# Weights of two modes in one load, and Q, K and V loaded in runs of 36 tokens

## The chip, the cores and the metric

The kernel runs on one core of a Trainium2 chip. The metric is the device time of one execution in microseconds (us); the kernel before has a median of 426.58 us over 9 runs (426.47 to 427.04). PE is TensorE (matmuls, and transposes made as matmuls), DVE is VectorE, ACT is ScalarE, POOL is GpSimd and SP is SyncE. In this kernel POOL issues all loads and SP most of the stores; the transfers themselves run on 16 DMA engines.

## The reference, cut to what matters

Inputs are q, k and v (8 batches, 8 heads, 576 tokens, 64 channels, fp32), the weights w_r and w_i (64 modes of 512x512, fp32) and w_ch (512x512). The first half is causal attention with a window of 64 tokens:

```python
scores = scale * np.matmul(q, k.transpose(0, 1, 3, 2))
mask = (rel >= 0) & (rel < window)          # rel: query position less key position, window 64
attn = softmax(where(mask, scores, -1e9))
x = np.matmul(attn, v)                       # then (batch, token, head*64 + channel)
```

The second half mixes the 64 lowest frequencies along the tokens with a complex weight for each, and then the channels:

```python
X = np.fft.rfft(x, axis=1)
Yr = einsum('bmd,mde->bme', Xr, w_r) - einsum('bmd,mde->bme', Xi, w_i)
Yi = einsum('bmd,mde->bme', Xr, w_i) + einsum('bmd,mde->bme', Xi, w_r)
y = np.fft.irfft(Y, n=S, axis=1)             # Y is zero from mode 64 on
u = x + y
return u + np.maximum(u @ w_ch, 0.0)
```

The weights are 127 matrices of 1 MiB in fp32 (mode 0 needs no imaginary one); they are cast to bf16 by the load, so that one takes 512 KB of SBUF, 4 KB in each partition.

## The kernel before, in words

**Attention** goes batch by batch. `load` (L95) brings K, Q or V of one batch into a raw tile with one DMA; a partition holds two runs of `RUN` = 18 tokens, one of a head in the first half of the heads and one of a head in the second. `transpose_units` (L205) makes twelve units of each batch: nine parts (three each for K, V and Q), in which PE transposes a third of the run's tokens into a PSUM tile `pst` and ACT or DVE copies it out (L218, L221), and three `vback` units that turn V back. PE's and POOL's orders are written out by hand here: for every window `w` come the scores (L291), the weighing of the window before (L316), the masks (L272) and in between the units that are due, three to a window, and the Fourier transforms of finished batches (`dft`, `dft_turn`).

**Loads during attention.** After a part has freed a raw tile, `refill` (L375) issues the raw load of two batches later, and with it one weight (`early`, L354). The first 5 weights (`LW`) go to the pool `wlate`, 13 more (`EW`) to `wearly`, and at the end 15 to tiles of attention that have come free (`spare`, L362). So 33 weights, those of modes 0 to 16, are issued before the modes begin.

**The modes.** `mode(m)` (L566) multiplies the transformed activations XQ of mode m with its real and then its imaginary weights, four matmuls of 512 columns each (L575), and after each half calls `refill_w` (L518), which takes places that have come free and issues the next weights into them with `load_w` (L110). Places are the five tiles of `wlate`, eight of `wmid` (`mids`, L494) that lie where attention's tiles lay and close again from mode 48 on, when their memory is wanted for the spectra `Y` (`batch_tile`, L705), one `wx` from mode 48 on, and three parts of `wy` from mode 54 on. A list `opens` says from which mode a place may be used, and its last field up to which. All loads stand in one queue behind POOL; a load waits there for the place that it fills, and for the landing of the load eight before it, whose semaphore it uses again.

From mode 17 to 47 PE has other work between the modes, the channel products `Z` (L597, L609). For modes 0 to 47 the order on PE is found by the planner of the framework; from mode 48 on it is by hand again, with the inverse transforms of the spectra (L724, L726) and the last four modes in another form (`last_mode`, L775). After the last weight, `YT2` is filled, turned, and the output rows are summed, rectified and stored (L885, L890, L908).

The softmax here doesn't subtract the row's maximum and nothing guards it: scores larger than these inputs give would overflow.

## Time and profile before

| What | Value |
|---|---|
| median of 9 runs | 426.58 us |
| the profiled execution's own time | 426.47 us |
| its span, first to last instruction | 424.7 us |
| mean granted clock of TensorE | 0.939 |
| PE busy | 360.1 us (85%) |
| DVE, ACT, POOL busy | 184.7, 171.5, 89.5 us |
| DMA packets | 28646, 91.98 MB |
| raw loads | 24 of 576 KB |
| weight loads | 127 of 512 KB |

The profile is of one execution, on one core. Its page lists busy times by engine, the span in 40 slices of 10.6 us each (GB/s is what the DMA engines wrote), the DMA queues, the chain of work that ended last, and the costliest groups of instructions. Further answers of the trace give who waited for whom (us in total, times, longest), the chain in order of time (start, length, what) and the timeline of an engine. [...] Landing records say when a load had arrived. The loads of all weights are issued at L115, and those of Q, K and V at L97.

### The profile page before, as it was taken

How to read it: one execution, taken by the hardware profiler on the slowest of the kernel's cores; microseconds unless marked ns; L12 is line 12 of the kernel's file. 1: busy time of each engine (PE TensorE's matmuls, PEld its weight loads, DVE VectorE, ACT ScalarE, POOL GpSimd, SP SyncE). 2: the span in 40 equal slices, each digit the busy share in tenths (PEclk: the TensorE clock that was granted, in tenths of full speed). 3: DMA queues.
4: the chain of work that ended last, by engine and by line, in shares of the span. 5: the costliest groups of instructions: out<-in, count | busy, mean ns of one | idle time of the engine just before them, and what ended most of it. 6: DMA issues, size and time to landing. Idle time of an engine off the chain costs nothing.

```text
span 424.7 us, 8859 instructions
## 1 busy us (share of the span) xinstructions
PE 360.1 (85%) x3762; PEld 219.6 (52%) x3772; DVE 184.7 (44%) x397; ACT 171.5 (40%) x314; POOL 89.5 (21%) x171
## 2 busy tenths in 40 slices
PE   6989998998998899467698979999858986589993
PEld 5655765665665465212265646555334443256682
DVE  5566756766764201404542422333113432140994
ACT  4585865866863311201132313122113332130993
POOL 7231231331122142222222222221222132200000
PEclk9999999999996699966799998999999999959998
DMA  8999999999999999999999999999999999994598
GB/s 144 212 213 212 214 212 214 213 213 213 214 214 213 214 213 262 212 213 214 212 215 213 215 212 214 213 213 214 212 215 213 214 213 214 214 212 100 189 387 333
DMA packets 28646, 91.98 MB, mean 217 GB/s; under 512 B 2832, under 2 KB 3088, under 8 KB 28608
## 3 DMA queue, kind: packets, MB, share of 16 engines
q0 software_dynamic: 25344, 81.80, 96.6%
q1 hardware_dynamic: 3120, 9.50, 5.8%
q8 instruction: 29, 0.48, 0.4%
q10 hardware_dynamic: 144, 0.13, 0.1%
q14 instruction: 9, 0.07, 0.0%
HBM read 162.53 MB, written 9.44 MB: 405 GB/s over the span
## 4 chain that ended last, share of the span: by engine, by line
DMA 48%; PE 37%; DVE 8%; issue 2%; ACT 2%; POOL 1%; DVEq 0%; POOLq 0%
DMA wt<-in_moe_w_r_dram 36%; DMA wt<-in_moe_w_i_dram 7%; PE pso L316 7%; PE pst L218 6%; DMA wch<-in_moe_w_ch_dram 4%; PE pso L885 4%; PE psv L235 3%; DVE x_sb L324 3%; PE psx L338 3%; PE pss L371 2%; PE pss L272 2%; PE psy L575 2%; PE pss L291 2%; DVE vT L59 2%; PE pso L769 1%
## 5 line engine op out<-in xcount | busy, mean ns | idle before, releaser
L575 PE MATMUL psy<-wt,XQ 128*32 128x512 bf16 (+1 forms) x404 | 96.1, 407 | 31.9 <-DMA wt<-in_moe_w_i_dram 17.1
L575 PEld LDWEIGHTS <-XQ 128*32 128x32 bf16 x476 | 48.5, 131 | 77.1 <-issue 57.1
L604 DVE CAST xT<-pxt 128x256 fp32r<-128x256 bf16 (+1 forms) x68 | 26.3, 434 | 53.6 <-PE pxt L597 33.8
L115 POOL DMA_DIRECT2D wt<-in_moe_w_r_dram x54 | 29.0, 538 | 93.2 <-DMA wt<-in_moe_w_r_dram 44.3
L611 ACT CAST Z<-psz 128x512 fp32r<-128x512 f32 x36 | 21.1, 587 | 66.4 <-PE psz L609 66.3
L115 POOL DMA_DIRECT2D wt<-in_moe_w_i_dram x52 | 27.9, 537 | 81.1 <-DMA wt<-in_moe_w_i_dram 43.6
L297 ACT ACTIVATE et<-pss 128x512 bf16<-128x512 f32 x72 | 39.2, 599 | 13.2 <-PE pss L291 13.2
L609 PE MATMUL psz<-wch,xT 128*128 128x512 f32 x144 | 42.2, 429 | 0.9 <-DVE xT L604 0.9
L316 PE MATMUL pso<-vt,et 128*64 128x65 bf16 (+1 forms) x576 | 34.0, 209 | 5.2 <-DVE x_sb L324 5.1
L609 PEld LDWEIGHTS psz<-wch,xT 128*128 128x128 f32 x144 | 27.1, 200 | 15.1 <-issue 8.8
L316 PEld LDWEIGHTS <-et 128*64 128x64 bf16 (+1 forms) x576 | 23.7, 113 | 17.2 <-issue 9.8
L59 DVE COPY x_sb<-psy 128x256 f32<-128x256 f32 x15 | 6.4, 424 | 57.0 <-PE psy L575 57.0
L324 DVE TENSOR_TENSOR x_sb<-pso,rcp 128x640 bf16<-128x640 f32 x32 | 26.3, 822 | 0.9
L58 ACT COPY x_sb<-psy 128x256 f32<-128x256 f32 x15 | 5.6, 374 | 50.5 <-DVE x_sb L59 50.5
L885 PE MATMUL pso<-Y,trigI 128*128 128x512 f32 x80 | 23.1, 403 | 0.1
L908 DVE TENSOR_TENSOR ot<-pso,x_sb 128x512 f32<-128x512 f32 x35 | 22.2, 685 | 1.5 <-PE pso L885 1.1
L272 PE MATMUL pss<-band,ident_bf 64*64 64x512 bf16 x136 | 20.2, 407 | 1.5 <-ACT et L297 1.5
L59 DVE CAST x_sb<-psj 128x512 bf16<-128x512 f32 x18 | 12.2, 688 | 21.2 <-PE psj L786 18.3
L59 DVE COPY vT<-pst 128x768 bf16<-128x768 bf16 x16 | 15.3, 958 | 13.0 <-PE pst L218 13.0
L890 ACT ACTIVATE pso<-pso 128x512 f32<-128x512 f32 x36 | 19.1, 596 | 0.0
L58 ACT CAST x_sb<-psj 128x512 bf16<-128x512 f32 x18 | 10.6, 586 | 19.6 <-PE psj L786 19.6
L885 PEld LDWEIGHTS pso<-Y,trigI 128*128 128x128 f32 x80 | 14.5, 188 | 5.5 <-ACT pso L890 1.7
(157 smaller groups left out, 506.4 us busy)
## 6 DMA issues: line engine op xcount, KB each, us to landing
wt<-in_moe_w_r_dram POOLq DMA_DIRECT2D x54, 512.0 KB, 19.1
wt<-in_moe_w_i_dram POOLq DMA_DIRECT2D x52, 512.0 KB, 19.1
out_dram<-ot SPq DMA_DIRECT2D x15, 512.0 KB, 4.1
rk<-in_k_dram POOLq DMA_DIRECT2D x8, 576.0 KB, 9.6
rq<-in_q_dram POOLq DMA_DIRECT2D x8, 576.0 KB, 13.6
rv<-in_v_dram POOLq DMA_DIRECT2D x8, 576.0 KB, 12.2
wy<-in_moe_w_r_dram POOLq DMA_DIRECT2D x3, 512.0 KB, 17.7
wy<-in_moe_w_i_dram POOLq DMA_DIRECT2D x3, 512.0 KB, 19.1
```

What stands on the lines that cost most here:

```text
L59: return nc.vector.tensor_copy(out=o, in_=i)
L115: nc.gpsimd.dma_start(out=wt, in_=src[m].rearrange("(p c) e -> p c e", c=NC))
L218: nc.tensor.transpose(out=ps[64 * hh:64 * hh + 64, c, :], in_=src[:, hh, (c0 + c) * D:(c0 + c + 1) * D], identity=ident_bf)
L272: nc.tensor.matmul(out=pss[(2 * w + hh) % 3][64 * half:64 * half + 64, :], lhsT=ident_bf[pp, pp], rhs=view(band[pp], 128 * half, [[0, WIN ...
L297: nc.scalar.activation(out=et[:, hh, :], in_=pss[(2 * w + hh) % 3], func=ACT_F.Exp, scale=EX_SCALE)
L316: nc.tensor.matmul(out=pso[po, hh, (i // 2) * VW:(i // 2) * VW + D + 1], lhsT=et[pk, hh, col:col + 64], rhs=vt[pk, 1 - f % 2, 2 * hh + g / ...
L324: nc.vector.tensor_tensor(out=view(x_sb, b * NT * DM + g * D, [[4 * D, 2], [DM, NT], [1, D]]), in0=view(pso, 0, [[512, 2], [VW, NT], [1, D]]),
L575: nc.tensor.matmul(out=psy[r0:r0 + k, :], lhsT=xq(c, m, im, [[NM, k]]), rhs=w[:, c, :], start=(im + c == 0), stop=(im == (m > 0) and c == ...
L604: nc.vector.tensor_copy(out=xT[:, :, w * k:w * k + w], in_=view(psts[k], j, [[128, NC], [n, w]] if n > 1 else [[128, NC], [1, 64], [64, 2]]))
L609: nc.tensor.matmul(out=psz, lhsT=xT[:, c, :], rhs=wch[:, c, :], start=(c == 0), stop=(c == NC - 1))
L885: nc.tensor.matmul(out=tps[n], lhsT=trigI[:, tr:tr + 128], rhs=pair_tile(what, bb), start=False, stop=stop and r0 + k == 128, skip_group_c ...
L908: nc.vector.tensor_tensor(out=ot[:, j], in0=ps, in1=x_sb[:, b, t, :], op=ALU.add)
```

## The change

`RUN` becomes 36 tokens, so that a partition holds one run of one head, 64 partitions the first four heads and 64 the others; a batch of K is one block of memory read from end to end. A part still covers a third of the run, now `CP` = 12 tokens, with a transpose of 64 partitions by 64 channels for each token and half of the heads, 24 in place of 12.

The pool `wlate` is cut into two double places `WP` and a single one `W1`, and `wmid` into four double ones. `load_two` brings the weights of modes m and m+1 (both real, or both imaginary) in one DMA into a double place. The list `items` holds 30 such pairs for modes 17 to 46 and 34 single loads for modes 47 to 63. `refill_w` gives the next item the first free place that fits; a double place is split into two single ones when the next item is single. A pair's place comes free when the second of its modes is done. The tiles `Y` of the spectra are now shared by two batches.

```diff
-    RUN = S // 32
+    RUN = S // 16
+    CP = RUN // 3
...
+    WP = [wlate.tile([128, 2, NC, DM], BF16, name="wt", tag=f"wp{j}") for j in range(LW // 2)]
+    W1 = wlate.tile([128, NC, DM], BF16, name="wt", tag="w1")
...
-            out=r, in_=RAW[which][b].rearrange("(x g) (p c) d -> (g p) x (c d)", g=4, c=RUN))
+            out=r, in_=RAW[which][b].rearrange("h (p c) d -> (h p) (c d)", c=RUN))
...
+    def load_two(m, im, wt):
+        src = moe_w_i if im else moe_w_r
+        nc.gpsimd.dma_start(out=wt, in_=src[m:m + 2].rearrange("m (p c) e -> p m c e", c=NC))
+        for j in range(2):
+            wtiles[m + j, im] = wt[:, j]
...
-                ps = ps_misc.tile([128, 6, 128], BF16, name="pst", tag="misc")
-                for c in range(6):
+                ps = ps_misc.tile([128, CP, 64], BF16, name="pst", tag="misc")
+                for c in range(CP):
                     for hh in range(2):
-                        nc.tensor.transpose(out=ps[64 * hh:64 * hh + 64, c, :],
-                                            in_=src[:, hh, (c0 + c) * D:(c0 + c + 1) * D],
-                                            identity=ident_bf)
-                evac(view(dst, c0, [[S, 4], [RUN, 32], [1, 6]]),
-                     view(ps, 0, [[32, 4], [1, 32], [128, 6]]), on_act)
+                        pp = slice(64 * hh, 64 * hh + 64)
+                        nc.tensor.transpose(out=ps[pp, c, :], in_=src[pp, (c0 + c) * D:(c0 + c + 1) * D],
+                                            identity=ident_bf[pp, pp])
+                evac(view(dst, c0, [[S, 4], [RUN, 16], [1, CP]]),
+                     view(ps, 0, [[16, 4], [1, 16], [64, CP]]), on_act)
...
-    MW = 8
+    MW = 4
-    mids = {j: wmid.tile([128, NC, DM], BF16, name="wt", tag=f"wm{j}") for j in range(MW)}
+    mids = [wmid.tile([128, 2, NC, DM], BF16, name="wt", tag=f"wm{j}") for j in range(MW)]
...
+    M2, M1 = mode_of(nw), M0 - 1
+    items = [(m, im, True) for m in range(M2, M1, 2) for im in range(2)]
+    items += [(m, im, False) for m in range(M1, NM) for im in range(2)]
+    for j, wt in enumerate(WP):
+        opens.setdefault(mode_of(2 * j + 1), []).append((wt, True, NM))
+    opens.setdefault(mode_of(LW - 1), []).append((W1, False, ME - 3))
+    for j, wt in enumerate(mids):
+        at = mode_of(LW + EW + 1 - 2 * j) if j else vt_mode
+        opens.setdefault(at, []).append((wt, True, M0 + 2 * j))
...
+        while items:
+            m1, im1, two = items[0]
+            fit = [s for s in free if (s[1] or not two) and s[2] > m1 + two]
+            if not fit:
+                break
+            wt, pair, last = slot = fit[0]
+            at = free.index(slot)
+            free.pop(at)
+            items.pop(0)
+            if two:
+                load_two(m1, im1, wt)
+                slot_of[m1 + 1, im1] = slot
                 continue
+            if pair:
+                free.insert(at, (wt[:, 1], False, last))
+                slot = (wt[:, 0], False, last)
+            load_w(2 * m1 - 1 + im1, None, None, slot[0])
+            slot_of[m1, im1] = slot
...
-            Yp[b] = wmid.tile([128, 2, DM], FP32R, name=f"Y{b}", tag=f"wm{b}")
+            Yp[p] = wmid.tile([128, 2, 2, DM], FP32R, name=f"Y{p}", tag=f"wm{p}")
```

## The prediction

> **What bounds the kernel now.** I read the page's busy times, slices and queues first, then the waits, then the chain of work in order of time, then POOL's and PE's timelines.

> ```profile
> span 424.7 us, 8859 instructions
> GB/s 144 212 213 212 214 212 214 213 213 213 214 214 213 214 213 262 212 213 214 212 215 213 215 212 214 213 213 214 212 215 213 214 213 214 214 212 100 189 387 333
> q0 software_dynamic: 25344, 81.80, 96.6%
> q8 instruction: 29, 0.48, 0.4%
> HBM read 162.53 MB, written 9.44 MB: 405 GB/s over the span
> ```

> From slice 2 to slice 36 the loads write 212 to 215 GB/s without a break (the 262 is the one load that isn't cast). They read fp32 and write bf16, so that is some 427 GB/s read. By the landing records the first raw load lands at 6.76 us, the last weight at 389.94. No other engine is as full: PE is busy 85%.

> Next, the waits of POOL, which issues all the loads, and pieces of the chain (start, length, what):

> ```profile
> POOL wt L115 <- DMA wt<-in_moe_w_r_dram: 53.3, 26, 3.9
> POOL wt L115 <- DMA wt<-in_moe_w_i_dram: 50.8, 27, 3.8
> POOL wt L115 <- PE psy L575: 43.9, 18, 6.5
> ...
> 170.73 18.98 DMA wt<-in_moe_w_r_dram
> 314.08 19.14 DMA wt<-in_moe_w_r_dram
> 350.90 19.13 DMA wt<-in_moe_w_i_dram
> 370.08 1.88 PE psy L575 x4
> 390.21 0.49 PE psl L775 x16
> ```

> POOL mostly waits for the landing of the load eight issues back, not for a free place; about 19 us of transfers stand queued. The end is set so: the stream of loads to 389.9, then 34.8 us of work on PE, DVE and ACT after the last weight. A change counts if it alters the stream's rate, lets it run dry, or alters that tail.

> **Where it could run dry** is the handover from attention to modes:

> ```profile
> 141.48 0.54 POOL L115 DMA_DIRECT2D vt<-in_moe_w_i_dram  x1
> 148.51 0.53 POOL L115 DMA_DIRECT2D wt<-in_moe_w_r_dram  x1 [6.50 <-PE psy L575]
> ```

> The load of 141.48 lands at 155.26. A load's first byte needs about 2.7 us after issue (the first load: issued 1.25, landed 6.76, its transfer 2.78), so the one issued at 148.51 was ready by 151.2: 4.05 us of slack. In attention the raw loads wait on transposes, with slack of 3.4 us (issued 23.81, the one ahead landing at 29.91) and 3.6 us (39.53, 45.79) at the tightest.

> [...]from a 128x64 transpose to a 64x64 score 149 ns pass between starts, of which the 128 columns need 53, so some 95 ns a switch. [...]

> **The change part by part.**

> *Raw loads.* 24 loads go from 256 packets of 2304 B to 128 of 4608 B. Single packets took 192 ns (2304 B) and 324 ns (4096 B): the line through both has 22 ns fixed. But packets overlap: all together fill 410 us of an engine (96.6% of the span) in 386 us of stream. By landings a raw load alone takes 2.783 us for 576 KB, a weight load 2.458 us for 512 KB: only 0.65% more a byte. Removing that: 24 x 2.783 x 0.0065 = -0.43 us. Bounds: 0, and 192 x 22 ns = -4.3 us if each fixed part counted in full. I take -0.4.

> *First load.* POOL's first raw issue takes 0.83 us, a weight's 0.53; half the packets should start the stream about 0.2 us sooner (0 to -0.4).

> *Pairs.* Modes 17 to 46 have 60 loads; they become 30. Bytes and packets (two of 4096 B a partition) stay; 30 completions of 22 ns go: -0.66 in full, -0.15 if they overlap as data does; I take -0.3. Two packets a partition is the shape of the raw loads, which ran at full rate.

> *More PE instructions.* A part has 24 transposes instead of 12: 8 batches x 9 parts x 12 x 2 (weight load and matmul) = 1728 more. The 7534 PE records and q8's 0.48 MB give 64 B each, so 0.11 MB, 7 fetches of 16 KB more. One holds a DMA engine 0.61 us (16,384 B at 26.7 GB/s); their times repeat in a cycle of eight, so I take eight engines in turn: 7/8 x 0.61 = +0.5 us on the slowest (0 to +0.6).

> Stream: -0.4 - 0.2 - 0.3 + 0.5 = -0.4 us.

> *Transposes on PE.* The pace of matmuls with 64-column weights (start, length, engine, what):

> ```profile
> 46.76 0.41 PE L291 MATMUL pss<-qT,kT 64*64 64x128 bf16 x15
> 47.10 0.44 PE L316 MATMUL pso<-vt,et 128*64 128x65 bf16 x14
> 59.15 0.84 PE L218 MATMUL pst<-ident_bf,rq 128*64 128x128 bf16 x24
> ```

> The 24 transposes of the last line are two parts, 12 pairs whose halves run side by side; 0.62 us from first to last start is 56 ns a pair, set by 128 columns. After, two parts are 24 pairs of 64 columns. The weighing matmuls L316 (65 columns, two column halves) are nearest: the second pair comes 53 ns after the first[...], later pairs 29 to 36, mean 32. So 53 + 22 x 32 + 27 = 784 ns against 11 x 56 + 53 = 669: +115 ns, x 36 = +4.1 us over attention. Against it, 64x64 is the shape of scores (L291) and masks (L272). Taking PE's order of before and giving L218 the new shape, mode switches fall from 316 to 292: 24 x 95 ns = -2.3 us. Evacuations wait for the last matmul, whose modelled length falls from 219 to about 194 ns: 36 x 25 = -0.9. Net +0.9 us. Bounds: pairs at 28 ns (the scores' mean) give 36 x 27 ns - 3.2 = -2.2; at 53 ns always, 36 x 605 ns - 3.2 = +18.6.

> What hides +0.9 is the slack of 4.05 us. The change takes 1.0 of it, since the first refill opens after mode 1's imaginary half, not mode 0, and the quicker stream 0.6: 2.5 us are left. Beyond that each us is a us of the end. Evacuations keep 768 elements a partition (813 ns ACT, 958 DVE); I put them at nothing, between -0.1 and +0.1 us each, with the same cover.

> *Places.* Modes 17 to 46 have six double places, where before there were 13 single ones; W1 stands idle till mode 47. Every load now waits on a place, so the question is the queue's depth. PE's worst lag: weights of mode 32 (imaginary) landed at 236.4, were done at 246.5. With pairs the four next pair loads and one issued at 238.7 would be queued or landed, to 261: 14.5 us, less 2.7 of latency, is 11.8 us of slack. From mode 47 the counts are the old ones (4 + 1 + 1 + 3), where the tightest issue (337.36, the one ahead landing at 347.92) had 7.9 us. So nothing, covered by queue depth; each us beyond would cost a us.

> *Tail.* The shared Y tiles are written before either batch of a pair is read in it; its instructions stay. Nothing.

> Sum: 424.7 - 0.4 = 424.3; around the span lie 1.8 us (426.47 profiled); the median is 0.11 above: 426.2 us.

> **Rivals.** *Slower: transposes.* If two pairs' weight loads don't overlap ([...]the first pair of each L316 run speaks for it, later pairs against), attention ends 18.6 us later and the stream stands dry for 16: 442. At 40 ns a pair: +291 ns x 36 - 3.2 = 7.3, less 2.5: +4.8, 431. It decides from 35.5 ns a pair: net +3.8 us, 2.5 covered, 0.4 won elsewhere. Chance 0.24, of it 0.08 near 442.

> *Slower: pairs starve.* Weights arrive every 4.9 us instead of 2.46, PE idles longer in between, its clock may fall (it was 0.5 in four stretches of 3.4 to 6.8 us between 182 and 257), and lag at mode 32 may exceed the slack, or a slow stretch of 10 us shifts into the tail (5 us). 428 to 431; against: 11.8 us of slack. Chance 0.14.

> *Faster: packets count.* With the 22 ns in full: -4.3 - 0.7 - 0.2 + 0.5 = -4.7: 421.9; halfway 424. Against: raw and weight loads differ by 0.65% a byte. Chance 0.20, mostly 424 to 425.7.

> *Forecast*, stream unchanged: 0.42, itself 425.7 to 427.4.

> **Numbers.** 0.2%, 0.85 us, is about what a measurement of this kernel can tell from no change. Faster 0.20, same 0.42, slower 0.24 + 0.14 = 0.38. The range 424.6 to 433 leaves out the full packet win and the far transposes, 0.17.

> **What would show it.** q0 with 6144 fewer data packets of 2304 B, 3072 of 4608 B and no slice under 210 GB/s before the end: right. Raw loads landing every 2.76 us or less. L218 pairs at 32 ns; above 35 the slower rival. First pair load issued near 149.5; if later than 152.5, the stream broke there. A POOL wait on PE in modes 17 to 46 followed by a gap in GB/s would mean the places were too few. I am wrong if the tail after the last landing isn't 34.8 us.

## The result, and the profile after

The changed kernel takes 451.23 us (median of 10 runs, 446.93 to 452.22) against 426.64 us (31 runs of the kernel before). The ratio is 1.0554, 95% interval [1.0534, 1.0574]: 5.5% slower, where 426.2 us was forecast. The profiled execution took 446.53 us, just below the fastest of the ten; its span is 444.7 us, 20.0 us more than before. All that follows is set against this execution; what the median run loses beyond its 20.0 us no trace shows. In it the transposes of the parts are line 228 (218 before), the scores 300 (291), the masks 275 and 281 (266 and 272), the weighing 325 (316), the pair loads 123 and the mode's matmuls 593 (575).

Two rows of the page before, the granted clock and the chain that ended last:

```profile
PEclk9999999999996699966799998999999999959998
...
DMA 48%; PE 37%; DVE 8%; issue 2%; ACT 2%; POOL 1%; DVEq 0%; POOLq 0%
```

The page of the kernel after:

```profile
span 444.7 us, 10506 instructions
...
PEclk9996978998888959995659999999999999899998
...
GB/s 152 214 214 205 156 197 192 136 202 198 213 199 99 148 210 209 259 214 214 214 214 215 214 214 214 214 214 214 215 214 213 213 213 214 214 213 146 157 383 328
...
q0 software_dynamic: 21792, 81.80, 92.6%
...
q8 instruction: 36, 0.59, 0.5%
...
DMA 39%; PE 33%; issue 15%; DVE 7%; POOL 2%; ACT 2%; SPq 0%; POOLq 0%; DVEq 0%
```

The stream of loads, unbroken before, now has holes in slices 4 to 14, which is attention; from slice 18 to 36, where the pair loads are, it runs at 213 to 215 GB/s. So the pair loads never let the stream run dry. In the chain, "issue" has grown from 2% to 15%. POOL's timeline (start, length, what, idle time before it and its releaser) has the first pair load 22 us later than the 149.5 us forecast:

```profile
164.80 0.54 POOL L118 DMA_DIRECT2D vt<-in_moe_w_i_dram  x1
171.70 0.71 POOL L123 DMA_DIRECT2D wt<-in_moe_w_r_dram  x1 [6.37 <-PE psy L593]
```

The first matmul of a mode starts at 170.3 us, before at 147.1: attention ends 23.2 us late. The last weight lands at 409.5 instead of 389.94 (+19.6), and the rest, 35.2 us against 34.8, makes the 20.0. The question is what costs attention 23.2 us.

**PE stands still with nothing to wait for.** PE's waits, after (line, what it waited for: us in total, times, longest):

```profile
PE pst L228 <- issue: 7.1, 6, 1.9
...
PE pss L275 <- issue: 2.3, 1, 2.3
PE pss L300 <- issue: 2.1, 1, 2.1
PE psv L244 <- issue: 2.0, 2, 1.3
```

"issue" is time in which the engine waited for nothing that the profile shows. Before, the same four kinds of instruction had one such entry, 0.6 us at the scores. In PE's timeline it falls in the middle of a run of equal transposes, whose operands are all there:

```profile
51.99 0.60 PE L228 MATMUL pst<-ident_bf,rq 64*64 64x64 bf16 x26
54.03 0.44 PE L228 MATMUL pst<-ident_bf,rq 64*64 64x64 bf16 x16 [1.45 <-issue]
```

Nine such stops between 26 and 145 us, of 0.6 to 2.5 us from start to start, add up to 15.0 us. What they have in common is a count. PE's records (matmuls and weight loads) up to each stop, from the trace:

```
stop at us      26.0  32.3  52.4  69.7  91.8  97.7 109.0 127.0 144.0
length us        2.3   2.5   1.6   2.1   1.5   1.6   0.9   1.8   0.6
records so far   961  1217  1984  2751  3774  4030  4541  5308  6075
mod 256          193   193   192   191   190   190   189   188   187
```

Every distance is a multiple of 256 but for a record that is missing from the trace now and then. A packet of queue 8, which the page calls "instruction", has 16 KB (16384 B), and the 36 of them come to 63.7 bytes for each of the trace's 9262 PE records: 256 instructions of 64 bytes fill one packet. At seven of the nine stops such a packet starts within 1 us of PE's last record (26.1, 32.5, 51.7, 69.3, 91.0, 97.0, 126.5 us) and takes 0.89 to 0.97 us; at the other two it starts some 1.6 us sooner (107.4, 142.3). At all nine PE starts again 1.3 to 1.6 us after the packet's end. So PE comes to the end of a block of its own program before the next one is there. The blocks come all through the span, their packets between 13.1 and 417.4 us.

Counting packets along with records shows when a fetch begins. Counted in order, the packet before each of the nine restarts brings just the block that PE is short of, so each packet brings the block after the one that PE is in, and it starts some 3 us after PE has entered that one. At the stop of 52.4 us, PE enters the block at 48.5, the packet starts at 51.7 and ends at 52.7, and PE goes on at 54.0, 5.5 us after the entry; but PE was through with the block after 3.9. The nine blocks that end in a stop take PE 3.0 to 4.5 us.

The kernel before was already near that edge: its blocks in attention take 5.0 us and more, mostly about 6. It has one such stop, at record 1983, behind the block of 5.0 us:

```profile
59.91 0.39 PE L291 MATMUL pss<-qT,kT 64*64 64x64 bf16 x15
60.87 0.24 PE L291 MATMUL pss<-qT,kT 64*64 64x128 bf16 x3 [0.57 <-issue]
```

**The rate.** PE's work by stretch of attention (from:to, length, busy us and count of PE, PEld, DVE, ACT and POOL, granted clock, DMA share, GB/s), before and then after:

```profile
24.00:52.00 28.00, 26.84 (x569) 17.85 (x567) 19.17 (x35) 19.85 (x34) 7.37 (x12) 1.00 1.10 213
52.00:75.00 23.00, 21.05 (x456) 13.77 (x453) 14.27 (x24) 14.85 (x25) 5.15 (x9) 1.00 1.09 213
```

```profile
24.00:52.00 28.00, 23.17 (x577) 15.52 (x576) 14.37 (x24) 15.12 (x26) 4.94 (x10) 0.88 0.95 189
52.00:75.00 23.00, 18.92 (x477) 13.29 (x478) 11.32 (x19) 12.42 (x21) 4.24 (x8) 0.79 1.03 198
```

PE issues nearly the same number of instructions per stretch as before, although each batch now has 216 more, and DVE and ACT get less done: PE's instructions per microsecond hardly grow.

**The clock falls after stops.** In the trace it is at 0.5 for 34.5 to 41.3, 54.9 to 61.8, 72.0 to 75.4 and 99.3 to 102.7 us, each from within 1 us of the end of a stop of 1.5 to 2.5 us, and in three later stretches; up to the first mode 30.7 us more than before, which had 13.7 us of it at the end of attention, without a stop. The stops at 26.0 and 91.8 us, of 2.3 and 1.5 us, brought no fall. Stops of 15.0 us leave some 8 of the 23.2; I put them down to the clock by its place in time. That is argued, not shown: no run separates them.

### The profile page after: what moved, and what is told of

Read it like the earlier page. It is cut to its first block, busy times and chain, and to the rows that moved or that the text cites. A ratio compares the mean times of both kernels' runs of the same rounds, so it can differ in the third digit from the quotient of the medians.

```text
span 444.7 us, 10506 instructions
## 1 busy us (share of the span) xinstructions
PE 356.1 (80%) x4626; PEld 225.9 (51%) x4636; DVE 184.4 (41%) x397; ACT 171.9 (39%) x314; POOL 74.5 (17%) x141
## 3 DMA queue, kind: packets, MB, share of 16 engines
q0 software_dynamic: 21792, 81.80, 92.6%
HBM read 162.53 MB, written 9.44 MB: 387 GB/s over the span
## 4 chain that ended last, share of the span: by engine, by line
DMA 39%; PE 33%; issue 15%; DVE 7%; POOL 2%; ACT 2%; SPq 0%; POOLq 0%; DVEq 0%
DMA wt<-in_moe_w_r_dram 21%; DMA wt<-in_moe_w_i_dram 13%; PE pst L228 7%; PE pso L325 6%; PE psv L244 4%; DMA wy<-in_moe_w_i_dram 4%; PE pso L904 2%; DVE x_sb L333 2%; PE pss L382 2%; PE pss L281 2%; PE psx L347 2%; PE pss L300 2%; PE psy L593 2%; DVE ot L927 2%; DVE vT L60 1%
## 5 line engine op out<-in xcount | busy, mean ns | idle before, releaser
L593 PE MATMUL psy<-wt,XQ 128*32 128x512 bf16 (+1 forms) x404 | 83.5, 415 | 39.6 <-DMA wt<-in_moe_w_i_dram 27.2
L593 PEld LDWEIGHTS <-XQ 128*32 128x32 bf16 (+1 forms) x476 | 46.2, 132 | 79.3 <-issue 61.4
L627 PE MATMUL psz<-wch,xT 128*128 128x512 f32 x144 | 40.3, 417 | 0.4 <-DVE xT L622 0.4
L325 PE MATMUL pso<-vt,et 128*64 128x65 bf16 (+1 forms) x576 | 35.7, 215 | 5.4 <-DVE x_sb L333 5.4
L325 PEld LDWEIGHTS <-et 128*64 128x64 bf16 (+1 forms) x576 | 24.9, 118 | 17.6 <-issue 11.8
L627 PEld LDWEIGHTS psz<-wch,xT 128*128 128x128 f32 x144 | 26.0, 193 | 11.6 <-issue 5.7
L123 POOL DMA_DIRECT2D wt<-in_moe_w_r_dram x15 | 10.7, 715 | 74.2 <-PE psy L593 67.6
L281 PE MATMUL pss<-band,ident_bf 64*64 64x512 bf16 x136 | 21.2, 455 | 1.5 <-ACT et L306 1.5
L300 PE MATMUL pss<-qT,kT 64*64 64x128 bf16 (+1 forms) x640 | 20.1, 228 | 2.1 <-issue 2.1
L244 PE MATMUL psv<-ident_bf,vT 128*128 128x128 bf16 (+1 forms) x160 | 18.9, 259 | 2.1 <-issue 2.0
L118 POOL DMA_DIRECT2D wt<-in_moe_w_r_dram x25 | 13.4, 538 | 32.8 <-DMA wt<-in_moe_w_r_dram 15.3
```

The lines of the kernel that those rows point to most:

```text
L244: nc.tensor.transpose(out=ps[r0:r0 + n, i, :], in_=vT[:, g, t0:t0 + n], identity=ident_bf)
L281: nc.tensor.matmul(out=pss[(2 * w + hh) % 3][64 * half:64 * half + 64, :], lhsT=ident_bf[pp, pp], rhs=view(band[pp], 128 * half, [[0, WIN ...
L300: nc.tensor.matmul(out=pss[(2 * w + hh) % 3][64 * half:64 * half + 64, col:col + nq], lhsT=kTs[b % 2][pp, g, 64 * kb:64 * kb + 64], rhs=qT ...
L325: nc.tensor.matmul(out=pso[po, hh, (i // 2) * VW:(i // 2) * VW + D + 1], lhsT=et[pk, hh, col:col + 64], rhs=vt[pk, 1 - f % 2, 2 * hh + g / ...
L593: nc.tensor.matmul(out=psy[r0:r0 + k, :], lhsT=xq(c, m, im, [[NM, k]]), rhs=w[:, c, :], start=(im + c == 0), stop=(im == (m > 0) and c == ...
L627: nc.tensor.matmul(out=psz, lhsT=xT[:, c, :], rhs=wch[:, c, :], start=(c == 0), stop=(c == NC - 1))
```

## The experiments

Two theories stood at the start: that PE runs out of instructions because there are more of them (any 1728 more would do it), and that the new transposes or the new loads themselves cost the time (their form, the wait on a 36-token tile, the pair places). The first four kernels were compared with the kernel before on one chip (426.61 us, 39 runs), the last three on another (426.63 us, 7 runs).

**The 36-token runs alone.** The kernel after with the single weights and places of the kernel before:

```diff
-    wlate = wl.enter_context(tc.tile_pool(name="wlate", bufs=1))
+    wlate = wl.enter_context(tc.tile_pool(name="wlate", bufs=LW))
...
-    MW = 4
+    MW = 8
```

> The raw loads in runs of 36 tokens and their 24 transposes a part, with the weights loaded one by one as before. Theory, instruction supply: PE stops at the ends of 16 KB blocks of its own instructions (256 of them), because in attention it now takes them faster than they are fetched beside the loads; 1728 more instructions come with the transposes, so all of the loss is here: attention ends near 170 us instead of 147, 446 to 453 us. Rival, places: double places leave the stream short; then this kernel is at 426 to 428. Rival, tile form: transposes of 64x64 are slow by themselves; then it is at 446 to 453 too, but without stops at block ends.

449.54 us, ratio 1.0526 [1.0485, 1.0567]. Ten stops, the first at records 961, 1217, 1985 and 2753 as in the kernel after; the first mode starts at 174.0 us. As far as four runs can tell, the whole loss is in the 36-token runs.

**The pair loads alone.** Raw loads and transposes as before, weights 17 to 46 in pairs:

```diff
+    def load_two(m, im, wt):
+        src = moe_w_i if im else moe_w_r
+        nc.gpsimd.dma_start(out=wt, in_=src[m:m + 2].rearrange("m (p c) e -> p m c e", c=NC))
...
-    MW = 8
+    MW = 4
```

> The weights of modes 17 to 46 two modes in a load, with the raw loads and transposes as before. Instruction supply: no more instructions in attention, so 426.0 to 427.5 us, attention ending at 147 us. Places: the loss is here, 440 us or more, with GB/s under 210 in modes 17 to 46.

426.16 us, ratio 0.9992 [0.9984, 1.0000]; no stop. Its slices:

```profile
GB/s 144 212 214 212 213 213 212 213 214 211 215 212 214 214 213 262 214 216 214 213 216 214 213 216 214 213 215 214 214 214 212 214 212 215 212 214 95 197 384 328
```

The last weight lands at 389.3 us, 0.6 sooner than before. The pairs cost nothing; the half microsecond that they seem to win lies at the edge of the interval.

**More instructions without the change.** The kernel before, in which each mask of windows 6 and on is written in eight matmuls of 64 columns instead of one of 512: as many columns, the same loads, 1904 more PE instructions (weight loads and matmuls):

```diff
+            for c, hh in ((c, hh) for c in range(0, WIN, 64) for hh in pair if w >= 6):
+                for half in range(2):
+                    pp = slice(64 * hh, 64 * hh + 64)
+                    nc.tensor.matmul(out=pss[(2 * w + hh) % 3][64 * half:64 * half + 64, c:c + 64],
+                                     lhsT=ident_bf[pp, pp], rhs=band[pp, half, c % 128:c % 128 + 64],
+                                     start=True, stop=False, skip_group_check=True)
             for hh in pair:
+                if w >= 6:
+                    break
```

> The kernel before with each mask matmul of 512 columns from window 6 on cut into eight of 64 columns: the same loads, the same transposes, the same result, 1904 more instructions on PE and about 1.5 us more of PE time. Instruction supply: stops of 1 to 2.5 us at every few blocks of 256 as in the changed kernel, attention ending 18 to 28 us later, 443 to 455 us. Tile form, load layout, places: none of them is touched, so 426 to 428.5 us.

(The output of this kernel is not that of the kernel before, against what was expected of it, so only its time is read. DVE, ACT and POOL do as many instructions as before: 397, 314 and 171.) 450.81 us, ratio 1.0575 [1.0558, 1.0593]. Its waits, and a stop in PE's timeline:

```profile
PE pss L266 <- issue: 10.1, 7, 2.6
PE pst L218 <- issue: 6.0, 3, 2.2
```

```profile
63.07 0.74 PE L266 MATMUL pss<-band,ident_bf 64*64 64x64 bf16 x29
65.92 0.22 PE L266 MATMUL pss<-band,ident_bf 64*64 64x64 bf16 x3 [2.12 <-issue]
```

The first mode starts at 171.7 us. The stops are now mostly in the masks, at records 1217, 1473, 1985, 2241, 2753, 3521, 3777, 4545, 4801 and 6593, all multiples of 256 apart. Nothing of the change is in this kernel, and it loses as much: 24.2 us, where the change loses 24.6. This is the run that decides between the theories.

**The change with a sixth of its added instructions.** The kernel after with every second transpose left out and, in each part, two matmuls of 384 columns in their place: 288 PE instructions more than before, not 1728. Loads, pairs and PE tiling are as in the change. Half of the tokens are missing from the attention, so only the time is read:

```diff
-                for c in range(CP):
+                for hh in range(2):
+                    pp = slice(64 * hh, 64 * hh + 64)
+                    nc.tensor.matmul(out=view(ps.bitcast(FP32)[pp], 0, [[1, 384]]), lhsT=ident_bf[pp, pp],
+                                     rhs=view(src[pp], c0 * D, [[1, 384]]), start=True, stop=True)
+                for c in range(0, CP, 2):
```

> The changed kernel with every second transpose left out and one pair of matmuls of 384 columns for each part in their place: the same loads, double places and 64x64 form, about the same PE time, but only 288 instructions more than before instead of 1728. Half of the tokens of Q, K and V are left out of the attention, so only its time is read. Instruction supply: most stops go, attention ends by 152 us, 426 to 432 us. Tile form or load layout or places: it stays at 444 us or more.

427.31 us, ratio 1.0015 [0.9998, 1.0032], with two stops; PE's waits:

```profile
PE pst L232 <- issue: 1.1, 1, 1.1
PE pss L304 <- issue: 0.5, 1, 0.5
```

The first mode starts at 148.0 us, and the loss is gone with the instructions, though 36-token loads and pairs are all there and half of the 64x64 transposes too: a cost of each transpose by itself would have left about half of the loss.

**Does the load traffic hold the blocks back?** The kernel after with the early weights, which otherwise come one by one in batches 1 to 5, held to batch 6, so that the loads have pauses:

```diff
-        if b:
-            early(1)
```

> The changed kernel, but the weights that attention loads one by one beside Q, K and V are held back to batch 6, where all 18 are issued at once; till then the queue has the raw loads alone, about half of its traffic. Instruction supply with the fetch waiting behind the loads: up to window 21 (weights come from there on) PE hardly stops, and that window's exponential starts at 93 to 97 us (92.1 in the kernel before, 109.3 in the changed one). Instruction supply with a fetch time of its own, whatever the loads do: the stops stay, 106 us or more. The whole is slower than before either way, since the stream stands idle: 455 to 500 us.

459.94 us (two runs), ratio 1.0777 [1.0756, 1.0799]. Window 21's exponential is at 100.3 us, between the two values that would have decided. Its slices and waits:

```profile
GB/s 154 214 206 52 135 130 56 155 134 212 213 213 213 214 213 213 214 258 215 213 214 214 214 215 213 215 214 214 214 213 215 213 213 213 214 213 139 133 382 329
```

```profile
PE pst L228 <- issue: 3.4, 4, 1.5
PE pss L300 <- issue: 2.7, 1, 2.7
PE pss L275 <- issue: 0.9, 1, 0.9
```

Where the stream is thin, blocks follow each other in 3.5 to 4.7 us (54.7, 58.2; 64.6, 68.1; 79.5 to 100.7), and from 53 to 118 us no block end holds PE up for more than about 0.5 us; a stop of 2.9 us came at 25.9 us, before the traffic thinned. That speaks for the loads drawing the fetch out, but the kernel also got its raw loads late.

The traces of all nine kernels say more, by the time from PE's entry into a block to the start of the packet with the next one, between 24 us and the first mode. Where the DMA engines wrote 190 GB/s or more in that time, it has a median of 3.3 us and lies between 2.3 and 3.8 for four fifths of 157 packets. Where they wrote under 110 GB/s, it is at most 1.1 us for all 16. (20 packets fall between.) Both happen in one kernel: in the kernel after 3.2 us for the packet of 51.7 us, and 1.1 for that of 84.5, when the loads paused; the block that PE was in then took it 4.2 us and ended without a stop. So the fetch comes later under the loads; what holds it back among them, no trace shows.

**A third of the instructions.** The kernel before with K alone in 36-token runs (576 more PE instructions), and then with the pair loads as well:

```diff
+        if which == "k":
+            nc.gpsimd.dma_start(out=r, in_=k[b].rearrange("h (p c) d -> (h p) (c d)", c=RK))
...
-        return [part(rk, kT, 0, True), part(rk, kT, 6, False), part(rk, kT, 12, True),
+        return [part_k(rk, kT, 0, True), part_k(rk, kT, CP, False), part_k(rk, kT, 2 * CP, True),
```

> The kernel before with K alone in runs of 36 tokens: 576 more PE instructions, a third of the change's, and single weights. Instruction supply: a block of 256 lasts some 5.4 us instead of 6.1, about what its fetch needs, so a few short stops, attention 2 to 8 us longer, of which 3.7 are covered: 426 to 431 us. If the loss went with the form alone, a third of it: 434 us.

> K alone in runs of 36 tokens, and the double loads of modes 17 to 46. Instruction supply: as with K alone, less some 0.4 us for the pairs: 425.6 to 430.5 us. Places: nothing of it, above 434 us.

K alone: 431.2 us, ratio 1.0104 [1.0089, 1.0119], 0.2 above the range expected of it; three stops of over 0.6 us (records 1983, 3262, 3517), first mode at 154.3. With pairs: 432.72 us, ratio 1.0155 [1.0116, 1.0194], also above the range expected of it. Of its four runs two took 430.15 and 431.32 us, two 434.11 and 434.75; the profile is of the fastest and has five stops of 0.8 to 1.3 us. What the two slow ones lose isn't seen. The waits:

```profile
PE pst L234 <- issue: 1.5, 2, 0.9
PE pso L344 <- issue: 1.1, 2, 0.8
```

With K alone the first mode comes 7.2 us late, about a third of 23.2 us for a third of the instructions; the time grows by a fifth of the loss only, as the slack at the handover to the modes takes up the first microseconds.

The kernels side by side. "Wanted" is PE's records from 24 us to the first mode over the 123.1 us that the kernel before takes for this stretch; "got" is the same records over the stretch's own length:

```
kernel                      records  wanted/us  got/us  first mode us   time us
before                        4518      36.7     36.7       147.1        426.64
pairs alone                   4531      36.8     36.7       147.4        426.16
half the transposes           4773      38.8     38.5       148.0        427.31
K alone                       4954      40.2     38.0       154.3        431.20
K and pairs                   4910      39.9     38.0       153.1        432.72
after                         5943      48.3     40.6       170.3        451.23
36-token runs alone           5963      48.4     39.8       174.0        449.54
masks split                   6427      52.2     43.5       171.7        450.81
```

Up to some 39 records a microsecond PE gets nearly what it wants; from 40 on it falls behind, and it gets no more than 38 to 43.5 whatever it wants. These are means over attention. What stops PE is a single dense block: an estimate of what a fetch under the full stream needs is the median 3.3 us to its start, about 0.95 for the packet and 1.3 till PE goes on, some 5.5 us, or 46 records a microsecond within a block.

## Why the prediction was wrong

**The step that failed is "More PE instructions".** Its count was exact: 1728 instructions, and q8 went from 29 packets to 36, the 7 forecast. But it priced them only as 0.5 us of a DMA engine's time. Even that was small: a packet took 0.89 to 0.97 us in the trace of before, not the 0.61 that was the prediction's estimate from the 427 GB/s read over 16 engines. Above all it put at nothing that PE went on only with the next block there (at all nine stops 1.3 to 1.6 us after its packet's end), and that under this stream, by the estimate above, it could go on only some 5.5 us after entering a block. With the change attention wants 48 records a microsecond instead of 36.7, and its dense blocks last 3.0 to 4.5 us: stops of 15.0 us. The signs stood in the profile of before: each fetch starting 2.2 to 3.8 us after a block's entry, blocks that lasted little longer than the fetch, and an idle time on "issue" in the midst of equal scores.

**"Transposes on PE", net +0.9 us, failed for the same reason.** Its pace held: within a run, pairs start every 32 ns (the median of 856 in the trace of after), as it took from the weighing matmuls, and not every 53, as the first two pairs of those do; a transpose's record is mostly 193 ns long (194 forecast), six times the distance to the next, so that starts and not lengths tell the pace. Its terms for mode switches and evacuations were not measured by themselves: the 95 ns a switch were an estimate from the trace of before, the 149 ns between the starts of a transpose and the score behind it less the 53 from one pair of transposes to the next. What it forecast of attention, 0.9 us later, was 23.2: 15.0 in stops and some 8 more. (Its bound for pairs at 53 ns should be 577 ns and +17.6 us by its own formula, not 605 and +18.6; nothing hangs on it.)

**Slack.** Of the 23.2 us 3.6 were taken up before the stream's end; 2.5 were forecast.

**Stream, places, tail.** Where raw loads followed each other without a break, they landed every 2.76 us instead of 2.783, which would make -0.55 us if all 24 gained it, where -0.43 was forecast. The first load landed 0.02 us sooner, not 0.2. With pairs alone the stream ended 0.6 us sooner where their share was -0.3: right in sign, small as forecast. The places never starved the stream: POOL's waits moved from landings to places, as its waits after show, without a gap in GB/s.

```profile
POOL wt L123 <- PE psy L593: 102.8, 21, 9.1
```

The tail grew from 34.8 to 35.2 us, where nothing was forecast; the cause stays open.

**The rivals.** "Slower: transposes" had the place right (attention late, the stream dry, 442 us) and the cause wrong: at 32 ns a pair the weight loads, mostly 110 ns each in the trace, do overlap. "Pairs starve" is refuted by the pairs alone, and "packets count", for all but the small part forecast, by the raw loads' 2.76 us. That the gain is small rests on these landings.

## What to carry to other kernels

In this kernel PE's instructions had a supply as well as a duration: before splitting one operation into several short ones, count how long 256 of PE's instructions last in the densest stage, and compare that with the time from a block's entry to the end of the next fetch there (under this stream a median of 3.3 us to the packet's start and mostly 0.89 to 0.97 for the packet). Here blocks of about 6 us got through and those of 3 to 4.5 us stopped PE under the full stream; as a mean over attention, 37 to 39 instructions a microsecond got through, 40 began to cost, and at 48 and more PE fell 23 to 27 us behind. The distance between fetches alone doesn't tell the limit: in the kernel before, with one stop, packets started 5.9 to 7.5 us apart between 26 and 128 us, at PE's own pace, and in the kernel after, with nine, mostly 5.6 to 7.0. An idle time that waited for nothing, mostly in the middle of equal instructions and always a multiple of 256 records apart, was the sign of it here.
